# Half of w1's columns contracted in blocks of 128, 128, 96 and 96 rows, with the 96-row blocks loaded in eight transfers of 12 rows

## The chip, the cores and the metric

The kernel runs on one core of one Trainium2 chip. The metric is the device time of one execution in microseconds, the median of the runs. The profile is one further execution, taken by the hardware profiler; its times are microseconds from the first instruction of the program.

## What is computed

One decode step for a batch of two tokens of width 448. A gate mixes the result of a cached attention with that of a small two-layer network:

```python
# x (2,1,448); k_cache, v_cache (2,16,4096,256); w1 (448,1792); w2 (1792,448); all float32
g = sigmoid((x * gate_w).sum(-1, keepdims=True))
q = (x @ wq) in 16 heads of 256
p = softmax(q . k_cache / 16)            # over 4096 cached positions
a = (p . v_cache, heads joined) @ wo
b = maximum(x @ w1, 0) @ w2
out = g * a + (1 - g) * b
```

The two caches hold 268 MB of the 289.5 MB that an execution reads, and each of their values is used once.

## The kernel before

**The ring.** On-chip memory holds a ring of three slots of 16,384 floats in each of 128 partitions. There are 32 units, one for each batch entry and head. A unit's slot holds its K (16 KB x 2 per partition) and V (32 KB per partition). TensorE makes the scores (L131), VectorE takes their maximum (L351), ScalarE the exponentials (L318), and VectorE multiplies them into V in eight instructions (L356), the last of which raises `freed`. SyncE waits for `freed` and issues the load that reuses the slot, so a load is issued as soon as the unit that held its slot is done, some 19 us before its data are due.

**All loads are on SyncE's queue, in one order** (L67 to L178): `wq` with the small input `xg` behind it in slot 0, the units, and then, in slots that are free again, `wm` (w1 and w2) in slot 0 and `wo` in slot 1. `wm` is issued in two transfers, w1 (L170) and w2 (L171), once unit 29 is done; `wo` in six (L175), of 14, 8, 4, 3, 2 and 1 blocks of 448 columns, once unit 30 is done. Each transfer takes all 128 partitions and raises a semaphore of its own by 16.

**w1 in memory.** The 1,792 columns are four groups (g = 0 to 3) of 448. The 448 rows are contracted in three blocks of 128 and a rest of 64. The rest of two groups is stacked in one block of 128 partitions, which one matmul with the input `xl` (x in the upper half for one group, in the lower half for the other, zeros elsewhere) works off for both. So w1 is 14 blocks of 448 floats in each partition, 25,088 bytes, in two halves of seven: groups 0 and 1, then groups 2 and 3.

**The tail on TensorE** (`pe_tail`, L225 to L287) runs in this order: wait for w1 (L231); x times w1, contraction blocks 0 and 1 (`hidden(0, 2)`, recorded on L111, the helper `project`); wait for the last unit; two transposes of the softmax's maxima and sums (L234, L235), which start a chain on VectorE and ScalarE (L361 to L367); block 2 of w1; the weights of the four parts (L238); the rest of w1 (L114); the sum over the parts (L245); the hidden layer transposed (L250, L252); wait for w2, and 14 matmuls with it into `acc` (L258); then for each of the first three `wo` transfers a wait and its matmuls into `acc` (L270). VectorE copies `acc` out (L375), TensorE folds the copy into `z` (L278), adds the last three `wo` transfers there directly, a wait for each (L283), and VectorE copies `z` to `res` (L377), which SyncE stores (L178).

**The inputs of the first matmuls** are made by ScalarE from `xg` once `wq` has landed: `xr` (L297), `xn` (L298) and `xl` (L301). The last raises `x_ok`, for which TensorE's first instruction waits. `xg` is a few columns behind `wq` in the same rows: 4 blocks of 3 columns.

Of the kernel before, what the change touches and what calls it, by code (L numbers as in the profile page):

```python
# [4 lines left out]
AF = mybir.ActivationFunctionType  # L5
# [12 lines left out]

def gated_mix_decode(nc, wq, kv, wm, wo, out):
    U, _, SW = kv.shape  # L20
# [9 lines left out]
    HH = H // G  # L30
    NW = wq.shape[1] - KC * (B + 1)
    FG = 448
    NF = 14
    W1 = 2 * (2 * KF * FG + FG)
    DG = D // G
# [40 lines left out]
    xl = sb("xl", P, 2, RB, B)  # L76
    xn = sb("xn", P, P // B, B)
    ge = sb("ge", P, 1)
    gp = sb("gp", P, 1)
# [25 lines left out]
    def x_of(c, n=R):  # L105
        return xr[:, c].rearrange("p r b -> p (r b)")[:, :n]
# [10 lines left out]

    xg = slot[0][:, NW:wq.shape[1]].rearrange("p (c b) -> p c b", c=KC)

# [27 lines left out]
    w1 = slot[0][:, :W1]  # L147
    w2 = slot[0][:, W1:W1 + NF * D]
    w_o = slot[1]

    with nc.Block(no_gpsimd_drain=True) as block:

        @block.sync
        def _(_e):
            sp.wait_ge(q_mm, 2)
            sp.dma_start(slot[0], kv[2]).then_inc(slot_in[0], 16)
            with nc.Fori(0, LOOP - 2, engines=(ET.SP,)) as r:
                u0 = sp.snap(r * SLOTS)
                for k in range(SLOTS):
                    s = (k + 1) % SLOTS  # L160
                    sp.wait_ge(freed, u0 + k + 1)
                    sp.dma_start(slot[s], kv[bass.ds(u0 + k + SLOTS, 1)].rearrange("o p n -> (o p) n")  # L162
                                 ).then_inc(slot_in[s], 16)
            sp.wait_ge(freed, U - 4)
            sp.dma_start(slot[1], kv[U - 2]).then_inc(slot_in[1], 16)
            sp.wait_ge(freed, U - 3)
            sp.dma_start(slot[2][:, :SW // 2], kv[U - 1][:, :SW // 2]).then_inc(slot_in[2], 16)
            sp.dma_start(slot[2][:, SW // 2:], kv[U - 1][:, SW // 2:]).then_inc(last_v, 16)
            sp.wait_ge(freed, U - 2)
            sp.dma_start(w1, wm[:, :W1]).then_inc(w1_in, 16)  # L170
            sp.dma_start(w2, wm[:, W1:]).then_inc(w2_in, 16)  # L171
            sp.wait_ge(freed, U - 1)
            k = 0
            for n, s in zip(ACC + DIRECT, wo_in):
                sp.dma_start(w_o[:, k * D:(k + n) * D], wo[:, k * D:(k + n) * D]).then_inc(s, 16)  # L175
# [49 lines left out]
        def pe_tail():  # L225
            half = W1 // 2
            def hidden(lo, hi):
                return project(pa, w1, lambda c, g: g // 2 * half + (g % 2 * KF + c) * FG,
                               lambda i: i * half + 2 * KF * FG, FG, lo, hi)

            pe.wait_ge(w1_in, 16)  # L231
            hidden(0, 2)
# [62 lines left out]
        def _(_e):  # L295
            act.wait_ge(slot_in[0], 16)
            act.activation(xr, xg[:, :KF, None, :B].to_broadcast([P, KF, P // B, B]), AF.Copy)  # L297
            act.activation(xn, xg[:, KF:, :B].to_broadcast([P, P // B, B]), AF.Copy)  # L298
            act.wait_ge(xl_0, 1)
            for j in range(2):  # L300
                a = act.activation(xl[j * HP:(j + 1) * HP, j], xg[j * HP:(j + 1) * HP, KF:, :B]  # L301
                                   .to_broadcast([HP, RB, B]), AF.Copy)
# [135 lines left out]
```

## Time and profile before

| | |
|---|---|
| median of 3 runs | 676.2 us (675.98 to 676.47) |
| the profiled execution's own time | 676.38 us |
| its span, first to last instruction | 674.8 us |
| read from memory | 289.54 MB, 429 GB/s over the span |
| packets of the kernel's transfers, share of 16 DMA engines | 99.3% |
| VectorE, TensorE, ScalarE busy | 339.8, 213.0, 54.2 us |

The span leaves 1.6 us of the profiled execution's time outside it. In the profile, a name such as `ring<-in_wm` is a tile and what it is made from; `L170` is a line of the kernel; "128*32 128x448" is the shape of a weight load (128 partitions by 32 columns) and of what is streamed through it. A float32 matmul of the program is recorded as two. SPq rows are SyncE issuing a transfer. In brackets stands how long the engine was idle before, and whose end released it. DMA packets are the pieces that the 16 DMA engines move one after the other; a transfer also leaves a packet of a few bytes on each engine, which raises the semaphore.

### The profile page before, as it was taken

What the parts mean: (1) busy time and instruction counts of PE and PEld (TensorE: products, weight loads), DVE (VectorE), ACT (ScalarE), POOL (GpSimd) and SP (SyncE); (2) the same over time, 40 slices, a digit from 0 to 9 for tenths busy, and PEclk for the clock granted to TensorE, in tenths of its full rate; (3) what the DMA queues carried; (4) which work ended last, traced back from release to release, by engine and by line L of the source; (5) the groups of instructions that cost most, each with busy time, mean ns of one, the idle gap of its engine ahead of it and who ended that gap; (6) DMA issues with size and microseconds to landing.
All of it is one profiled execution on the core that took longest, in us unless ns stands there. A gap on an engine that the chain in (4) does not pass through costs nothing.

```text
span 674.8 us, 4173 instructions
## 1 busy us (share of the span) xinstructions
PE 213.0 (32%) x1279; PEld 52.0 (8%) x1279; DVE 339.8 (50%) x561; ACT 54.2 (8%) x144; POOL 1.1 (0%) x9
## 2 busy tenths in 40 slices
PE   0633221333332123333321233333222333332455
PEld 0210000000000000000000000000000000000011
DVE  0024566545455665544656654455566445456670
ACT  0110000000000000000000000000000000000110
POOL 0000000000000000000000000000000000000000
PEclk9976567767655676776656677665667767655879
DMA  9999999999999999999999999999999999999997
GB/s 381 427 435 436 435 435 435 435 435 435 435 435 435 435 435 435 435 435 435 431 435 435 435 435 435 435 435 435 435 435 435 435 435 435 435 435 406 420 437 304
DMA packets 6082, 289.59 MB, mean 429 GB/s; under 512 B 704, under 2 KB 832, under 8 KB 1216
## 3 DMA queue, kind: packets, MB, share of 16 engines
q1 hardware_dynamic: 6080, 289.55, 99.3%
q8 instruction: 2, 0.03, 0.0%
HBM read 289.54 MB, written 0.01 MB: 429 GB/s over the span
## 4 chain that ended last, share of the span: by engine, by line
DMA 70%; DVE 12%; PE 9%; issue 6%; DVEq 1%; ACT 1%; SPq 0%; ACTq 0%
DMA ring<-in_kv 65%; DVE ring L356 10%; PE sc L131 9%; DMA ring<-in_wo 4%; DVE nm L351 2%; DVEq L356 1%; ACT p L318 1%; PE z L283 0%; DVEq L348 0%; DVEq L353 0%; PE acc L270 0%; SPq L175 0%; SPq L162 0%; DVEq L351 0%; DVE a_sb L375 0%
## 5 line engine op out<-in xcount | busy, mean ns | idle before, releaser
L356 DVE SCALAR_TENSOR_TENSOR ring<-ring,p 128x1024 f32 x256 | 295.9, 1222 | 54.8 <-ACT p L318 54.8
L131 PE MATMUL sc<-ring,qc 128*32 128x512 f32 x1024 | 182.6, 878 | 417.8 <-DMA ring<-in_kv 417.8
L351 DVE TENSOR_REDUCE nm<-sc 128x1024 f32 x32 | 39.2, 1225 | 236.1 <-PE sc L131 236.1
L131 PEld LDWEIGHTS sc<-ring,qc 128*32 128x32 f32 x1024 | 41.2, 154 | 558.6 <-issue 558.6
L318 ACT ACTIVATE p<-sc,nm 128x1024 f32<-128x1024 f32 x32 | 35.7, 1114 | 257.8 <-DVE nm L351 257.8
L323 ACT ACTIVATE ov<-on 128x8 f32 x32 | 6.7, 208 | 309.0 <-DVE ring L356 309.0
L356 DVE DVE_READ_ACCUMULATOR ring<-ring,p 128x1 f32 x256 | 21.4, 83 | 0.0
L343 DVE TENSOR_SCALAR ge<-ge 128x1 f32<-128x1 f32 x1 | 0.2, 155 | 21.5 <-ACT ge L305 21.5
L196 PE MATMUL pa<-ring,xr 128*128 128x1 f32 x6 | 1.4, 356 | 21.4 <-ACT xl L301 21.4
L375 DVE COPY a_sb<-acc 128x448 f32<-128x448 f32 x1 | 0.6, 625 | 14.7 <-PE acc L270 14.7
L111 PE MATMUL pa<-ring,xr 128*32 128x448 f32 x24 | 4.2, 830 | 11.7 <-DMA ring<-in_wm 11.7
L270 PE MATMUL acc<-ring,oc 128*32 128x448 f32 x52 | 5.9, 544 | 4.7 <-DMA ring<-in_wo 4.7
L111 PE MATMUL pb<-ring,xr 128*32 128x512 f32 x48 | 7.1, 737 | 0.0
L318 ACT ACTIVATION_READ_ACCUMULATOR p<-sc,nm x32 | 6.2, 193 | 0.0
L320 ACT ACTIVATE qc<-qt x32 | 6.1, 192 | 0.0
L258 PE MATMUL acc<-ring,hr 128*32 128x448 f32 x28 | 3.2, 541 | 1.0 <-ACT hr L332 1.0
L196 PEld LDWEIGHTS pa<-ring,xr 128*128 128x128 f32 x6 | 1.4, 326 | 21.4 <-ACT xl L301 21.4
L270 PEld LDWEIGHTS acc<-ring,oc 128*32 128x32 f32 x52 | 1.7, 109 | 8.9 <-issue 5.9
L114 PE MATMUL pb<-ring,xl 128*64 128x512 f32 x8 | 2.2, 618 | 0.0
L297 ACT ACTIVATE xr<-ring 128x384 f32<-128x384 f32 x1 | 0.5, 522 | 18.3 <-DMA ring<-in_wq 18.3
L111 PEld LDWEIGHTS pb<-ring,xr 128*32 128x32 f32 x48 | 1.6, 132 | 3.9 <-issue 3.9
L308 ACT ACTIVATE q<-pb 128x512 f32<-128x512 f32 x2 | 1.2, 598 | 8.6 <-PE pb L114 8.6
(56 smaller groups left out, 23.7 us busy)
## 6 DMA issues: line engine op xcount, KB each, us to landing
ring<-in_kv SPq DMA_DIRECT2D x2, 4096.0 KB, 34.7
ring<-in_wq SPq DMA_DIRECT2D x1, 7174.0 KB, 19.5
ring<-in_wm SPq DMA_DIRECT2D x2, 3136.0 KB, 30.7
ring<-in_wo SPq DMA_DIRECT2D x1, 3136.0 KB, 24.4
ring<-in_wo SPq DMA_DIRECT2D x1, 1792.0 KB, 28.3
ring<-in_wo SPq DMA_DIRECT2D x1, 896.0 KB, 30.0
ring<-in_wo SPq DMA_DIRECT2D x1, 672.0 KB, 31.1
ring<-in_kv SPq DMA_DIRECT2D x31, 39.6
```

The costliest lines, as they stand in the source:

```text
L111: m = pe.matmul(dst[g * R:(g + 1) * R, :n], x_of(c), w[:, at(c, g):at(c, g) + n], start=(c == 0), stop=False)
L114: m = pe.matmul(dst[i * HP:(i + 1) * HP, :n], xl.rearrange("p j r b -> p (j r b)"), w[:, at_last(i):at_last(i) + n], start=False, stop=True)
L131: m = pe.matmul(sc[g * R:(g + 1) * R, c * CW:(c + 1) * CW], qc[:, s, t:t + 1].to_broadcast([P, R]), slot[s][:, lo:lo + CW], start=(t == 0) ...
L196: m = pe.matmul(pa[:, :1], x_of(c, P) if c < KF else xn[r].rearrange("p r b -> p (r b)"), xg[r, c, B:], start=(c == 0), stop=(c == KC - 1))
L258: pe.matmul(acc[g * R:(g + 1) * R, :D], hr[:, k, :], w2[:, k * D:(k + 1) * D], start=(k < G), stop=False)
L270: m = pe.matmul(acc[g * R:(g + 1) * R, :D], o_of(k), w_o[:, k * D:(k + 1) * D], start=False, stop=(k >= n - G))
L308: act.activation(q, pb, AF.Copy, scale=SCALE).then_inc(q_ok, 1)
L318: act.activation(p, sc, AF.Exp, bias=nm[:, bass.ds(u, 1)], accum_out=ls[:, bass.ds(u, 1)]).then_inc(raised, 1)
L320: act.activation(qf[:, bass.ds((u + 2) % SLOTS * T, T)], qt[:, bass.ds(u + 1, 1), :].rearrange("p o t -> p (o t)"), AF.Copy).then_inc(quer ...
L323: act.activation(ov[:, bass.ds(u, 1), :].rearrange("p o j -> p (o j)"), on, AF.Copy).then_inc(kept, 1)
L351: dve.tensor_reduce(nm[:, bass.ds(u, 1)], sc, axis=AX.X, op=ALU.max, negate=True).then_inc(maxed, 1)
L356: m = dve.scalar_tensor_tensor(v, v, 1.0, p, op0=ALU.mult, op1=ALU.mult, accum_out=on[:, j:j + 1])
```

## The change

Groups 0 and 1 stay as they were. For groups 2 and 3 the 448 rows are contracted as 128 + 128 + 96 + 96. The two blocks of 128 stay in `wm`; the 96-row blocks of both groups, four blocks of 448 floats in each of 96 partitions, become a new input `we`. It is loaded behind w1 in eight transfers: transfer j brings 12 rows of 7,168 bytes to the partitions j, j + 8, ..., j + 88. All nine transfers raise `w1_in`, and TensorE waits for all nine ahead of its first matmul with w1. The bytes in total stay the same: w1's row goes from 25,088 to 19,712 bytes in 128 partitions, and 96 rows of 7,168 bytes are added. In memory, the rows of `we` that go to the partitions 8r to 8r + 7 lie 44,800 bytes apart, which is also the new pitch of `wm`, and the next eight start 9 x 44,800 bytes on.

A matmul of a 96-row block streams 96 partitions. The contraction's second-last block is rows 256 to 351, which are in `xr` already; the last, rows 352 to 447, needs a new input tile `xe`. It is one more instruction on ScalarE ahead of `x_ok`, from three more columns of `xg`, so `wq`'s rows grow from 57,392 to 57,404 bytes.

```diff
-    NW = wq.shape[1] - KC * (B + 1)
+    NW = wq.shape[1] - (KC + 1) * (B + 1)
-    W1 = 2 * (2 * KF * FG + FG)
+    PS = 96
+    W1 = 2 * KF * FG + FG + 4 * FG
+    WE = 4 * FG
...
     w1 = slot[0][:, :W1]
-    w2 = slot[0][:, W1:W1 + NF * D]
+    w1e = slot[0][:PS, W1:W1 + WE]
+    w2 = slot[0][:, W1 + WE:W1 + WE + NF * D]
...
             sp.wait_ge(freed, U - 2)
             sp.dma_start(w1, wm[:, :W1]).then_inc(w1_in, 16)
+            for j in range(8):
+                sp.dma_start(w1e[j::8], we[:, j, :WE]).then_inc(w1_in, 16)
             sp.dma_start(w2, wm[:, W1:]).then_inc(w2_in, 16)
...
         def pe_tail():
-            half = W1 // 2
+            half = 2 * KF * FG + FG
+
             def hidden(lo, hi):
-                return project(pa, w1, lambda c, g: g // 2 * half + (g % 2 * KF + c) * FG,
-                               lambda i: i * half + 2 * KF * FG, FG, lo, hi)
-
-            pe.wait_ge(w1_in, 16)
+                for c in range(lo, hi):
+                    for g in range(G):
+                        i, h = divmod(g, 2)
+                        if i == 0 and c == KF:
+                            if g == 0:
+                                pe.matmul(pa[:HP, :FG], xl.rearrange("p j r b -> p (j r b)"),
+                                          w1[:, 2 * KF * FG:half], start=False, stop=True)
+                            continue
+                        x, at = x_of(c) if c < KF else xe.rearrange("p r b -> p (r b)"), (h * KF + c) * FG
+                        if i:
+                            at = half + (h * 2 + c) * FG if c < 2 else (h * 2 + c - 2) * FG
+                        w = w1e if i and c >= 2 else w1
+                        m = pe.matmul(pa[g * R:(g + 1) * R, :FG], x[:PS] if w is w1e else x, w[:, at:at + FG],
+                                      start=(c == 0), stop=(c == KC - 1))
+                return m
+
+            pe.wait_ge(w1_in, 9 * 16)
             hidden(0, 2)
...
             act.activation(xr, xg[:, :KF, None, :B].to_broadcast([P, KF, P // B, B]), AF.Copy)
-            act.activation(xn, xg[:, KF:, :B].to_broadcast([P, P // B, B]), AF.Copy)
+            act.activation(xn, xg[:, KF:KC, :B].to_broadcast([P, P // B, B]), AF.Copy)
+            act.activation(xe, xg[:, KC:, :B].to_broadcast([P, RB, B]), AF.Copy)
...
+    both = w1[:2 * P, 1].reshape(2, P, 2, FG).transpose(1, 2, 0, 3).reshape(P, -1)
+    rest = w1[2 * P:, 1].reshape(2, PS, 2, FG).transpose(1, 2, 0, 3).reshape(PS // 8, 8, -1)
+    we = np.zeros((PS // 8, 9, 25 * FG), np.float32)
+    we[:, :8, :rest.shape[2]] = rest
+    w1 = np.concatenate([full, last, both], 1)
```

More of the change, by code (lines that the diff above doesn't have):

```diff
@@ L16, with gated_mix_decode @@
 DIRECT = (3, 2, 1)
-def gated_mix_decode(nc, wq, kv, wm, wo, out):
+def gated_mix_decode(nc, wq, kv, wm, we, wo, out):
     U, _, SW = kv.shape
@@ L77, in gated_mix_decode @@
     xn = sb("xn", P, P // B, B)
+    xe = sb("xe", P, RB, B)
     ge = sb("ge", P, 1)
@@ L116, in project @@
         return m
-    xg = slot[0][:, NW:wq.shape[1]].rearrange("p (c b) -> p c b", c=KC)
+    xg = slot[0][:, NW:wq.shape[1]].rearrange("p (c b) -> p c b", c=KC + 1)
     ident_0, ident_ok, par_ok, fold_ok, xl_0 = (ev() for _ in range(5))
@@ L297, in _ @@
             act.activation(xr, xg[:, :KF, None, :B].to_broadcast([P, KF, P // B, B]), AF.Copy)
-            act.activation(xn, xg[:, KF:, :B].to_broadcast([P, P // B, B]), AF.Copy)
+            act.activation(xn, xg[:, KF:KC, :B].to_broadcast([P, P // B, B]), AF.Copy)
+            act.activation(xe, xg[:, KC:, :B].to_broadcast([P, RB, B]), AF.Copy)
             act.wait_ge(xl_0, 1)
             for j in range(2):
-                a = act.activation(xl[j * HP:(j + 1) * HP, j], xg[j * HP:(j + 1) * HP, KF:, :B]
+                a = act.activation(xl[j * HP:(j + 1) * HP, j], xg[j * HP:(j + 1) * HP, KF:KC, :B]
                                    .to_broadcast([HP, RB, B]), AF.Copy)
@@ L404 @@
     full, last = blocks(np.concatenate([np.asarray(A_x).reshape(B, D).T, np.asarray(gate_w).reshape(D, 1)], 1))
-    xg = np.concatenate([full, np.concatenate([last, last])[:, None]], 1)
+    PS = 96
+    ext = np.zeros((P, 1, B + 1), np.float32)
+    ext[:PS, 0] = np.concatenate([full[PS:, KF - 1], last])
+    xg = np.concatenate([full, np.concatenate([last, last])[:, None], ext], 1)
     kt = np.asarray(A_k_cache)[:, heads].reshape(B, H, S, T, P).transpose(1, 0, 4, 3, 2).reshape(U, P, T * S)
@@ L416 @@
     wo = np.asarray(A_wo).reshape(HH, G, R, J, D).transpose(1, 2, 0, 3, 4).reshape(P, -1)
-    full, last = blocks(B_w1)
-    full = full.reshape(P, KF, 2, 2, FG).transpose(0, 2, 3, 1, 4).reshape(P, 2, -1)
-    last = last.reshape(HP, 2, 2, FG).transpose(2, 0, 1, 3).reshape(P, 2, FG)
-    w1 = np.concatenate([full, last], 2).reshape(P, -1)
+    w1 = np.asarray(B_w1).reshape(D, 2, 2, FG)
+    full, last = blocks(w1[:, 0])
+    full = full.reshape(P, KF, 2, FG).transpose(0, 2, 1, 3).reshape(P, -1)
+    last = last.reshape(HP, 2, FG).transpose(1, 0, 2).reshape(P, FG)
+    both = w1[:2 * P, 1].reshape(2, P, 2, FG).transpose(1, 2, 0, 3).reshape(P, -1)
[3 more added lines that the diff above has]
+    w1 = np.concatenate([full, last, both], 1)
     w2 = np.asarray(B_w2).reshape(G, FG, D)
@@ L424 @@
     w2 = np.concatenate([full, last], 1).reshape(P, -1)
-    arrays = {"wq": wq, "kv": kv, "wm": np.concatenate([w1, w2], 1), "wo": wo}
+    arrays = {"wq": wq, "kv": kv, "wm": np.concatenate([w1, w2], 1), "we": we, "wo": wo}
     arrays = {n: np.ascontiguousarray(a) for n, a in arrays.items()}
```

## The prediction

> **What bounds the kernel now.** I read the page first (engines, slices, DMA packets, chain), then the chain of waits at the end, then windows over the last two microseconds.
>
> ```profile
> GB/s 381 427 435 436 435 435 435 435 435 435 435 435 435 435 435 435 435 435 435 431 435 435 435 435 435 435 435 435 435 435 435 435 435 435 435 435 406 420 437 304
> DMA packets 6082, 289.59 MB, mean 429 GB/s; under 512 B 704, under 2 KB 832, under 8 KB 1216
> q1 hardware_dynamic: 6080, 289.55, 99.3%
> DMA 70%; DVE 12%; PE 9%; issue 6%; DVEq 1%; ACT 1%; SPq 0%; ACTq 0%
> ```
>
> The transfers run without a gap: 99.3% of sixteen engines, 435 GB/s in nearly every slice, 27.2 GB/s for each engine. So the bytes that the busiest engine carries, and what follows its last one, set the time. The 6,080 packets also tell how a transfer is cut. There are 43 transfers; 42 of 128 rows and the output of 16 rows make 5,392 packets if a row is one packet, and 43 x 16 = 688 small ones raise the semaphores: 6,080. One row is one packet, on one engine.
>
> ```profile
> 639.02 29.95 DMA ring<-in_wo
> ...
> 669.02 1.00 PE acc L270 x8
> 670.02 0.02 issue
> 670.05 0.64 DVE a_sb L375
> 670.68 0.04 issue
> 670.73 0.40 PE z L278 x8
> 671.12 1.53 PE z L283 x48
> ```
>
> The end waits for transfers twice: for the third piece of `wo` (to 668.98), and inside the last group (L283) for the last pieces. If all pieces land earlier or later by the same amount, the end moves by that amount.
>
> ```profile
> core 0: us, PE busy (x) PEld busy (x) DVE busy (x) ACT busy (x) POOL busy (x), PEclk, DMA share, GB/s
> 16.87:320.00 303.13, 98.37 (x552) 24.06 (x552) 148.41 (x242) 25.10 (x67) 0.00 (x0) 0.67 1.01 435
> 670.00:670.50 0.50, 0.00 (x0) 0.00 (x0) 0.45 (x1) 0.00 (x0) 0.00 (x0) 1.00 0.64 244
> 670.50:671.40 0.90, 0.67 (x28) 0.68 (x32) 0.17 (x1) 0.00 (x0) 0.00 (x0) 1.00 0.12 48
> 671.40:672.00 0.60, 0.60 (x27) 0.37 (x20) 0.00 (x0) 0.00 (x0) 0.00 (x0) 1.00 0.05 18
> ```
>
> The DMA share is the number to look at. At 670.5 most engines have ended. Until 671.4 it is 0.12, two engines of sixteen; after that 0.05, one engine for the larger part of the window. So fourteen engines end near 670.5, one at 671.4, one at 671.9: the last one is 1.4 us late, and the kernel waits for it. What makes two engines late shows in the DMA view of two short windows, 60 to 66 us and 659 to 661.5 us, the only ones with a packet of another queue:
>
> ```profile
> q8 instruction: 1, 0.02, 1.0%
> ...
> q8 instruction: 1, 0.02, 2.4%
> ```
>
> Each is a fetch of instructions, 1.0% of 16 x 6 us and 2.4% of 16 x 2.5 us, so 0.96 us of one engine, and the data behind it moves back by that or more. Two fetches, two late engines: I take the one as the cause of the other. The view doesn't number the engines.
>
> **The change, part by part.**
>
> ```profile
> ring<-in_wo SPq DMA_DIRECT2D x1, 3136.0 KB, 24.4
> ring<-in_wo SPq DMA_DIRECT2D x1, 1792.0 KB, 28.3
> ring<-in_wo SPq DMA_DIRECT2D x1, 896.0 KB, 30.0
> 638.18 2.70 SPq L175 DMA_DIRECT2D ring<-in_wo  x6
> L170 SPq DMA_DIRECT2D ring<-in_wm x1: 328/328/328, 620.0 to 620.0; - x1
> L171 SPq DMA_DIRECT2D ring<-in_wm x1: 432/432/432, 620.4 to 620.4; - x1
> DMA to landing us min/median/max: 27.2/30.7/34.3
> ```
>
> *Bytes on each engine.* w1 and w2, 3,136 KB each, land (34.3 - 27.2) + 0.4 = 7.5 us apart. The 896 KB piece of `wo` has rows of 7,168 bytes, eight on each engine; it lands 30.0 - 28.3 plus the 0.43 us between two issues = 2.13 us behind the piece before it. w1 shrinks to 19,712 of 25,088 bytes: 7.45 x 0.214 = 1.6 us less on every engine. `we` is eight transfers of twelve packets. A transfer of twelve packets can use twelve engines at most. If it is always the same twelve, each gets eight rows of 7,168 bytes, +2.13 us, net +0.55 us, and the other four are left at -1.6 us. [...]
>
> *Do twelve rows land at full speed?* Every load in this trace fills all 128 partitions, so no row prices one that fills twelve. When only two engines are left (670.5 to 671.4) they move 48 GB/s, 24 each, with fourteen others idle: an engine doesn't get faster when the rest are silent. So the limit is a lane of its own, the engine or the place in on-chip memory where it writes, and the row can't say which. Lower bound: the engine is the limit, and a packet takes what the 896 KB piece shows, 2.13 us for eight. Upper bound: the place is the limit, and two rows of a transfer share one place: twice that, +2.13 us. I take a value near the upper end, +2.0 (engines are some tenths of a microsecond apart, as the 0.64 in 670.0 to 670.5 shows, and two that meet a little apart share a little less). What decides me is that the rate stands at 435 GB/s to within 1 in nearly every slice: every lane is full at both ends, with no spare seen in the place of landing. [...]
>
> *The end.* The twelve: 670.5 + 0.55 + 2.0 = 673.05. The two late engines, if both are among the spared four: 671.9 - 1.6 = 670.3, not last any more. The end moves by 673.05 - 671.9 = +1.2 us.
>
> *Work that hides.*
>
> ```profile
> SPq L175 <- DVE ring L356: 17.4, 1, 17.4
> 647.26 3.21 PE L111 MATMUL pa<-ring,xr 128*32 128x448 f32 x16 [11.73 <-DMA ring<-in_wm]
> 650.40 0.40 PE L234 MATMUL pc<-ident,nm 128*32 128x128 f32 x1
> 650.94 1.01 PE L111 MATMUL pa<-ring,xr 128*32 128x448 f32 x8
> 652.62 0.97 PE L114 MATMUL pa<-ring,xl 128*64 128x448 f32 x4
> 656.25 3.20 PE L258 MATMUL acc<-ring,hr 128*32 128x448 f32 x28 [1.01 <-ACT hr L332]
> 662.72 3.20 PE L270 MATMUL acc<-ring,oc 128*32 128x448 f32 x28 [3.27 <-DMA ring<-in_wo]
> 39.72 5.51 PE L131 MATMUL sc<-ring,qc 128*32 128x512 f32 x32 [4.65 <-DMA ring<-in_kv]
> 20.71 0.29 ACT L298 ACTIVATE xn<-ring 128x128 f32<-128x128 f32 x1
> ```
>
> Eight more issues on SyncE, 8 x 0.43 = 3.5 us, stand between w1 and w2 at 620; w2's data are due 25 us later, and the next thing on that queue is `wo`, ahead of which SyncE waits 17.4 us. Cost 0. If that wait were under 3.5 us, `wo` would be late by the difference.
>
> The wait of L231 now ends with the last row of `we`, 0.55 us later by bytes alone, 2.55 with shared landing, less what late engines had cost it: 647.3 becomes about 648.7. Behind it on TensorE are the 3.2 us of `hidden(0, 2)` and the two transposes (L234, L235) for which the softmax chain on VectorE and ScalarE waits; they move from 650.4 to some 652. `w2` lands up to 2.5 us later on the twelve engines, and before 657, about when the hidden layer is ready. The rest of w1 takes one more matmul, two records of 0.13 to 0.25 us (L111 x8 took 1.01, L114 x4 0.97), at most 0.5 us. In sum TensorE comes to L270 up to 2.2 us later, and there it has 3.27 us of idle time in front of `wo`, which itself moves by 1.2. Cost 0. Were that cover gone, the excess over 3.27 + 1.2 us would be added to the end.
>
> `xe` is one more ScalarE instruction, 0.2 to 0.3 us like L298, ahead of all of TensorE's work; the first unit then has 4.65 us to spare before its data. 12 bytes more in 57,392 cost nothing that can be seen.
>
> Sum against the profiled execution: 676.38 + 1.2 = 677.6. Its time is 0.18 above the median of 676.2, so the forecast is 677.4.
>
> **The rivals.**
>
> *Full speed, late engines spared.* The engine is the limit, and twelve rows land at full speed. The twelve end at 670.5 + 0.55 = 671.05, the spared late ones at 670.3: -0.85, of which extra semaphore packets (eight for one) take about 0.1. 675.45. For it: no row shows two engines disturbing each other. Against it: no row shows a lane with room. The case turns to the forecast when the eight packets take over 0.85 us more than 2.13.
>
> *Shared landing, and the last engine isn't spared.* The later of the two is one of the twelve: 671.9 + 0.55 + 2.0, +2.6 us, 678.8. For it: nothing numbers the late engines, and three in four are not spared if they fall anywhere. Against it: only that both fetches come over one queue, so that the two late engines may well be neighbours.
>
> *Full speed, the last engine isn't spared:* +0.55, 676.75.
>
> *The rows are dealt round all sixteen engines.* Then each gets six rows, as many bytes as before; the change moves nothing that counts: 676.2.
>
> **How the numbers follow.** The rule for twelve engines I give 0.93. Shared landing against full speed I put at about 2 to 1 in its favour. That the last engine is spared I put at over three quarters, above the one in four of a blind draw, because the two fetches came over one queue and so aren't two separate draws; no row carries that number, and it is the weakest step. So: shared and spared 0.48, full and spared 0.24, shared and not spared 0.15, full and not spared 0.06, dealt round 0.07.
>
> A measurement of this kernel tells about 0.2% from no change, 1.35 us: under 674.85 or over 677.55. The forecast lies 0.15 us inside; I count 0.43 of its 0.48 chance as slower, 0.21. With 0.14 of the third case, slower is 0.35. Faster needs more than the whole 1.4 us of lateness back: 0.04. The rest, 0.61, is within. The likeliest case's own range is 676.9 to 677.9. The range of 8 in 10 runs from 675.3 (full speed) to 678.6 (most of the case not spared).
>
> **What would show it.** In the windows of the changed kernel the DMA share stays high past 671.0 and falls in two steps, the pairs last, near 673. The GB/s row falls from 437 in its second-last slice (641 to 658), in which `we` lands. w1's wait ends near 648.7. If instead the share is near zero at 671.1, full speed holds; if one engine alone remains to 674, the last engine wasn't spared; if the end of transfers looks as before, 0.12 then 0.05, the rows were dealt round. An idle time before L270 that isn't released by `wo` would break the step that TensorE's tail is covered. A change over 3 us either way would mean a mechanism that I don't have.

## The result and the profile after

The changed kernel takes 679.37 us, median of 7 runs (677.19 to 680.71), beside 676.2 us (7 runs, 675.98 to 677.05) for the kernel before on the same chip. The ratio is 1.0043, with a 95% interval of 1.0028 to 1.0058: slower by about 2.9 us. The forecast was 677.4 us with a range up to 678.6.

The traced execution, however, came out nearly as forecast by its span: 675.7 us, 0.9 above the 674.8 of before (forecast +1.2). Its own time is 678.44 us, with 2.7 us outside the span where before's trace has 1.6. First the page of the changed kernel, the same rows that the prediction shows of before:

```profile
GB/s 381 431 434 432 434 434 434 434 434 434 434 434 434 434 434 434 434 434 434 434 434 434 434 434 434 434 434 434 434 434 434 434 434 434 434 434 433 422 380 326
DMA packets 6274, 289.59 MB, mean 429 GB/s; under 512 B 800, under 2 KB 928, under 8 KB 1408
q1 hardware_dynamic: 6272, 289.56, 99.4%
DMA 68%; DVE 12%; PE 11%; issue 6%; DVEq 1%; ACT 1%; SPq 0%; ACTq 0%
```

The second-last slice, where `we` lands, is down from 437 to 380 GB/s; the first 36 slices are within 4 GB/s of before. The 192 packets more are 96 rows and 8 times 12 semaphore packets. Twelve and not sixteen: there are 96 more under 512 B than before (800 for 704), so each of the eight transfers leaves twelve semaphore packets where one of 128 rows leaves sixteen. I read that as twelve engines.

Windows of the changed kernel, one before `we`, one in it, and four at the end (columns: busy time of each engine with the number of instructions, granted clock, DMA share, GB/s):

```profile
637.70:643.50 5.80, 0.00 (x0) 0.00 (x0) 4.09 (x8) 1.50 (x4) 0.00 (x0) 0.65 1.01 434
643.90:647.40 3.50, 0.00 (x0) 0.00 (x0) 3.50 (x7) 0.00 (x0) 0.00 (x0) 0.50 1.20 288
...
670.00:671.00 1.00, 0.87 (x8) 0.06 (x8) 0.06 (x1) 0.00 (x0) 0.00 (x0) 1.00 0.91 371
671.00:672.00 1.00, 0.39 (x16) 0.39 (x20) 0.56 (x1) 0.00 (x0) 0.00 (x0) 1.00 0.85 339
672.00:672.40 0.40, 0.40 (x26) 0.34 (x16) 0.00 (x0) 0.00 (x0) 0.00 (x0) 1.00 0.66 251
672.40:673.00 0.60, 0.60 (x24) 0.35 (x16) 0.00 (x0) 0.00 (x0) 0.00 (x0) 1.00 0.04 15
```

Read the last two columns together. A window counts a packet whole where it starts, so a share can pass 1; what tells is the rate for the busy share. It is 288 / 1.20 = 240 GB/s while `we` lands and 434 / 1.01 = 430 ahead of it: the packets take longer. This is what the prediction called shared landing. At the end, before had one or two engines left from 670.5 to 671.9; now most of them run to 672.4 and then stop, with one engine 0.3 us behind (0.04). So in this execution the late engines were spared, as forecast, and the twelve end last, at 672.4 instead of the forecast 673.05. Part of that is luck: the packets of the last unit ended some 0.4 us earlier in this execution than in before's trace.

The trace keeps every DMA packet with its start, length and size, and they say more than the windows. On one engine a packet starts within some 5 ns of the end of the one before it, so the packets can be sorted into sixteen chains, one for each engine. A row of `we` takes 272 ns on its engine at first, and 420 to 550 once all twelve engines are at it. But the four engines that carry no row of `we` slow down as well: their first packets of w2 take up to 1.78 us in place of 0.93. So the rows hinder other transfers too, and not only each other two by two within one, as the prediction had it. By this the two late engines, forecast to end at 670.3, end at 671.6 and 671.9, as late as in before; they are only not the last any more.

The tail on TensorE and the third piece of `wo`, from the timeline of the changed kernel:

```profile
648.98 3.21 PE L247 MATMUL pa<-ring,xr 128*32 128x448 f32 x16 [14.09 <-DMA ring<-in_we]
...
663.64 3.20 PE L290 MATMUL acc<-ring,oc 128*32 128x448 f32 x28 [1.59 <-DMA ring<-in_wo]
667.78 1.71 PE L290 MATMUL acc<-ring,oc 128*32 128x448 f32 x16 [0.94 <-DMA ring<-in_wo]
669.91 0.96 PE L290 MATMUL acc<-ring,oc 128*32 128x448 f32 x8 [0.42 <-DMA ring<-in_wo]
...
673.61 0.28 DVE L398 COPY res<-z 128x112 f32<-128x112 f32 x1 [2.05 <-PE z L303]
```

w1 is ready at 648.98 (forecast 648.7, before 647.26). The idle time ahead of `wo` shrinks from 3.27 to 1.59 us but is still ended by `wo`: TensorE's tail stays covered. The third piece starts at 669.91 instead of 669.02, 0.89 us later, and what follows it takes as long as before (to 673.61, +0.93 against 672.68). That is the whole difference of the traced spans.

Most of the other executions are longer than the traced one. The spans of the seven runs are 675.7 (traced), 677.7, 675.5, 678.8, 677.5, 678.0 and 679.1 us. So the question for the experiments was not what the trace shows, but what makes five executions of seven 1.8 to 3.4 us longer than it.

### The profile page after: what moved, and what is told of

It is laid out like the page before. It is cut to its first block, busy times and chain, and to the rows that moved or that the text cites. A ratio compares the mean times of both kernels' runs of the same rounds, so it can differ in the third digit from the quotient of the medians.

```text
span 675.7 us, 4186 instructions
## 1 busy us (share of the span) xinstructions
PE 214.6 (32%) x1281; PEld 52.4 (8%) x1281; DVE 339.8 (50%) x561; ACT 54.3 (8%) x145; POOL 1.1 (0%) x9
## 3 DMA queue, kind: packets, MB, share of 16 engines
q1 hardware_dynamic: 6272, 289.56, 99.4%
## 4 chain that ended last, share of the span: by engine, by line
DMA 68%; DVE 12%; PE 11%; issue 6%; DVEq 1%; ACT 1%; SPq 0%; ACTq 0%
DMA ring<-in_kv 64%; PE sc L134 10%; DVE ring L377 10%; DMA ring<-in_wo 4%; DVE nm L372 2%; DVEq L377 1%; ACT p L339 1%; PE z L303 0%; DVEq L369 0%; DVEq L374 0%; PE acc L290 0%; SPq L181 0%; SPq L166 0%; DVEq L372 0%; DVE a_sb L396 0%
## 5 line engine op out<-in xcount | busy, mean ns | idle before, releaser
L247 PE MATMUL pa<-ring,xr 128*32 128x448 f32 (+1 forms) x24 | 4.4, 854 | 14.1 <-DMA ring<-in_we 14.1
L290 PE MATMUL acc<-ring,oc 128*32 128x448 f32 x52 | 5.9, 544 | 2.9 <-DMA ring<-in_wo 2.9
L290 PEld LDWEIGHTS acc<-ring,oc 128*32 128x32 f32 x52 | 1.7, 109 | 7.1 <-issue 4.2
L393 DVE COPY oc<-pc 128x256 f32<-128x256 f32 x4 | 1.4, 416 | 1.5 <-PE pc L265 1.5
```

Of the source, the lines that this page charges most:

```text
L247: m = pe.matmul(pa[g * R:(g + 1) * R, :FG], x[:PS] if w is w1e else x, w[:, at:at + FG], start=(c == 0), stop=(c == KC - 1))
L290: m = pe.matmul(acc[g * R:(g + 1) * R, :D], o_of(k), w_o[:, k * D:(k + 1) * D], start=False, stop=(k >= n - G))
```

## The experiments

Four explanations were tried against each other. The expectations number or letter them as they came up, and put them in words: that landing is shared and the late engines are spared in every execution (the forecast); that the late engines sit on other engines from one execution to the next, so that the credit for sparing them is earned in some executions alone (called Theory 4 later on); that shared landing itself scatters; and that the cost isn't in the loads at all but in TensorE's longer program, through a third fetch of instructions near the end (called Theory A). Each row of the table is one kernel beside the kernel before on the same chip; "third piece" is the start of the third `wo` group in the timeline of its trace, and "idle" the idle time ahead of the first, as in the rows above. The kernel before had medians of 676.2 to 676.5 us on these chips.

| kernel | median us (range, runs) | ratio, 95% interval | w1 ready | idle | third piece | traced span |
|---|---|---|---|---|---|---|
| before | 676.2 (675.98 to 677.05, 7) | | 647.26 | 3.27 | 669.02 | 674.8 |
| the changed kernel | 679.37 (677.19 to 680.71, 7) | 1.0043 (1.0028 to 1.0058) | 648.98 | 1.59 | 669.91 | 675.7 |
| again | 680.21 (678.19 to 681.18, 6) | 1.0054 (1.0042 to 1.0066) | 648.94 | 1.72 | 670.00 | 676.9 |
| one96 | 679.3 (678.19 to 680.24, 5) | 1.004 (1.0027 to 1.0053) | 649.06 | 1.25 | 670.00 | 675.8 |
| nine | 678.62 (676.64 to 679.77, 12) | 1.0027 (1.0017 to 1.0038) | 648.27 | 0.22 | 669.31 | 675.1 |
| before_plus | 676.18 (675.79 to 676.96, 11) | 0.9999 (0.999 to 1.0008) | 646.96 | 1.53 | 668.57 | 674.3 |
| after_short | 680.23 (677.52 to 680.97, 6) | 1.0051 (1.0036 to 1.0066) | 649.02 | 1.73 | 670.02 | 675.9 |
| nine_short | 678.55 (676.86 to 679.77, 7) | 1.0031 (1.002 to 1.0042) | 648.35 | 0.34 | 669.41 | 675.2 |
| one96_short | 678.57 (677.77 to 679.02, 6) | 1.0031 (1.0019 to 1.0043) | 649.36 | 0.16 | 670.28 | 676.5 |
| native64 | 676.64 (675.3 to 678.45, 11) | 1.0008 (0.9997 to 1.0018) | 647.58 | 1.31 | 668.57 | 674.4 |
| shared64 | 677.73 (676.33 to 681.73, 12) | 1.0029 (1.0013 to 1.0045) | 648.10 | 1.39 | 669.27 | 675.3 |
| contig12 | 680.3 (678.88 to 681.53, 5) | 1.0066 (1.0053 to 1.0079) | 650.49 | none | 671.47 | 677.3 |
| before_xe | 676.66 (675.94 to 677.53, 11) | 1.0006 (0.9997 to 1.0015) | 646.98 | 3.24 | 668.70 | 674.5 |

### The changed kernel once more (again, again2)

No edit. It tells how firm the result is on another chip, and whether another trace shows the same end.

> The changed kernel once more, for its scatter (677.2 to 680.7 us in seven runs; the kernel before 676.0 to 677.1). Theory 1, shared landing and late engines: the twelve engines are slowed in the same way each time, and the time depends on whether the two late engines (behind a fetch of instructions) are among the four spared: levels near 677.2, and 1.4 and 2.8 us above it. Theory 2, shared landing alone: the slowing itself differs from run to run, so no levels, and in a slow execution all twelve engines end late together.

> The changed kernel, for a second trace. Theory 1: if its span is over 677, one engine alone ends last, 1 us or more behind the rest. Theory 2: if its span is over 677, the twelve engines end together and the window of the 12-row transfers is longer than the 3.5 us of the first trace.

The ratio is 1.0054: the cost is there again, and larger. The spans are 676.9 (traced), 677.2, 678.9, 677.4, 677.7 and 678.1 us. The second trace, again2, is one execution of 677.93 us with a span of 675.5. In both traces the third piece starts at 670.00 and 669.62, as in the first: three traces in three show a short execution. In the trace of again, the DMA view of the last stretch (674.0 to 676.9 us) has a packet of the other queue, which in the first trace comes only after the last instruction, at 677.4 us:

```profile
q8 instruction: 1, 0.02, 2.0%
...
out<-res SPq DMA_DIRECT2D x1, 7.0 KB, 2.8
```

2.0% of 16 x 2.9 us is 0.93 us of one engine. It is a third fetch of instructions; the store of the output, which took 1.8 us in the first trace, takes 2.8 here behind it. That is 1.0 of the 1.2 to 1.4 us by which this span is longer than the first's and again2's, and it gave Theory A.

### One transfer of 96 rows (one96)

```diff
-            for j in range(8):
-                sp.dma_start(w1e[j::8], we[:, j, :WE]).then_inc(w1_in, 16)
+            sp.dma_start(w1e, we).then_inc(w1_in, 16)
...
-            pe.wait_ge(w1_in, 9 * 16)
+            pe.wait_ge(w1_in, 2 * 16)
```

Sixteen engines with six rows each: the bytes on each engine are those of before, and everything else is the change.

> The same matmuls, but the 96 rows in one transfer, so that all sixteen engines take six rows each. Theory 1 and 2: no engine has more bytes than before, and rows of different engines meet less, so 676.2 to 676.8 us and a scatter as small as before. Rival, the contraction itself costs (one more matmul, xe, the later wait): still 677.5 us or more.

A miss: 679.3, as slow as the changed kernel. Its timeline shows w1 ready as late as there:

```profile
649.06 3.21 PE L246 MATMUL pa<-ring,xr 128*32 128x448 f32 x16 [13.86 <-DMA ring<-in_we]
```

So 96 partitions are dear even when sixteen engines carry them. The run shows that the bytes alone don't explain the cost; what makes 96 partitions dear isn't shown. Here no engine is spared (the DMA share is 1.00 from 670 to 671 us), and the late ones are last again, with two engines left after the others:

```profile
671.60:672.70 1.10, 0.97 (x33) 0.74 (x33) 0.05 (x1) 0.00 (x0) 0.00 (x0) 1.00 0.12 49
```

### Twelve rows nine partitions apart (nine)

```diff
-    PS = 96
+    PS = 107
...
-                sp.dma_start(w1e[j::8], we[:, j, :WE]).then_inc(w1_in, 16)
+                sp.dma_start(w1e[j:j + 100:9], we[:, j, :WE]).then_inc(w1_in, 16)
...
-            act.activation(xe, xg[:, KC:, :B].to_broadcast([P, RB, B]), AF.Copy)
+            act.activation(xe, xg[:, KC:, None, :B].to_broadcast([P, 2, RB, B]), AF.Copy)
```

The same twelve engines and bytes; rows r and r + 4 are now 36 partitions apart instead of 32. The inputs `xe` have zeros in the partitions between.

> Eight transfers of 12 rows as in the change, the same twelve engines and bytes, but partitions nine apart (j, j + 9, ...), with x placed to match and zeros between. If two rows of a transfer share a landing place at a distance of 32 partitions, this parts them: a packet takes its 272 ns, the window of these rows moves over 380 GB/s in place of 288, and the end comes 1.5 to 2 us earlier than with the change: 675.4 us where the late engines are spared, 676.8 where one is not. If the number of engines alone decides, the time is that of the change, 679.4.

678.62: 0.75 us below the first measurement of the changed kernel, 1.6 below again on the same chip, and 2.1 above before. w1 is ready 0.71 us earlier (648.27). Half a step: the distance matters, and it isn't the whole. The twelve spans fall in two heaps: 675.0 to 675.7 us (five, the traced one among them) and 676.5 to 678.5 (seven). That is what a cost would look like that is there in some executions and not in others.

### Is it TensorE's program? (before_plus, after_short, nine_short, one96_short)

To the kernel before, one product is added whose result the next one overwrites, so that its program gets longer:

```diff
             hidden(2, KF)
+            pe.matmul(z[:R, :FG], x_of(0), w1[:, :FG], start=True, stop=True)
             pe.wait_ge(wb_ok, 1)
```

And from three kernels six instructions of TensorE are taken out (the tile `hs` is widened to 512 columns, and ScalarE fills the new ones with one instruction more):

```diff
-            for t in range(KF):
-                pe.transpose(pb[:, t * P:(t + 1) * P], hs[:, t * P:(t + 1) * P], ident)
-            for j in range(2):
-                m = pe.matmul(pb[j * HP:(j + 1) * HP, KF * P:], hs[:, KF * P:], ident, start=True, stop=True)
+            for t in range(KC):
+                m = pe.transpose(pb[:, t * P:(t + 1) * P], hs[:, t * P:(t + 1) * P], ident)
```

> The kernel before, with one matmul more in TensorE's tail (four instructions: two weight loads, two matmuls), whose product is overwritten; loads as before. Theory A, length of TensorE's program: the change's extra matmul makes it long enough that a third page of instructions is fetched at the end, as the traces of all the changed kernels have it (674.8 to 677.4 us) and that of before has not; then this one has the third fetch, 677.5 to 680 us and a scatter of 3 us. Theory B, the loads of the 96 rows cost all: two fetches, 676.5 us.

> The change with TensorE's program made six instructions shorter, two fewer than before: two matmuls that transpose the hidden layer's last columns are replaced by one transpose, with a second ScalarE instruction that writes these columns twice. Theory A: no third fetch, and what is left is the price of the twelve engines that share landing places, +0.9 us by the first trace: 677.2 us, scatter under 1.5 us. Theory B: no difference to the change, 679.4 to 680.2.

> Partitions nine apart and the shorter program. Theory A: no third fetch, and the span of the first trace with nine apart (675.1) less nothing: 676.5 us, within 0.2% of before. Theory B: as nine apart alone, 678.6.

> All 96 rows in one transfer over sixteen engines and the shorter program. Theory A: 676.2 to 677 us, as before. Theory B: as one transfer alone, 679.3.

before_plus costs nothing (0.9999, 0.999 to 1.0008), though its trace does have the third fetch. The DMA view from 675.0 to 676.8 us, of the longer program:

```profile
DMA packets 1, 0.02 MB, mean 9 GB/s; under 512 B 0, under 2 KB 0, under 8 KB 0
...
q8 instruction: 1, 0.02, 3.3%
```

It comes here behind the output's store and delays nobody. And the three shortened kernels are as slow as their originals: 680.23, 678.55 and 678.57 beside 679.37, 678.62 and 679.3, all with ratios of 1.003 to 1.005. But taking out six instructions did not take out the third fetch: all three traces still have it. The DMA view of after_short from 672 to 680 us:

```profile
q8 instruction: 1, 0.02, 1.1%
```

So these three kernels don't try Theory A. What speaks against it as the whole cost is before_plus, and the loads alone further down, which have no fetch and cost nearly as much more (+2.56 us). That a third fetch which comes early costs some executions 1 us, as in again, stays.

### The same engines and bytes, rows four and eight partitions apart (native64, shared64)

Groups 2 and 3 are contracted as 128, 128, 128 and 64 rows. The 64 rows of 3,584 bytes come in eight transfers of eight rows, so eight engines carry 1.05 us more and w1 takes 0.53 less on all. The two kernels differ in one line, the distance of the rows of a transfer, four or eight partitions (and in the order of the rows in memory):

```diff
-                sp.dma_start(w1e[j // 4 * 32 + j % 4:j // 4 * 32 + j % 4 + 29:4], we[:, j, :WE]).then_inc(w1_in, 16)
+                sp.dma_start(w1e[j::8], we[:, j, :WE]).then_inc(w1_in, 16)
```

> Another split: groups 2 and 3 contracted as 128, 128, 128 and 64, the 64 rows (of 3,584 bytes) loaded in eight transfers of 8 rows four partitions apart. Eight engines carry 0.57 us more, eight 0.53 us less, and no two rows of a transfer lie 32 partitions apart. Theory 3, where landing places are shared the slowing is large and uneven, and that is the scatter: here nothing is shared, so 675.6 to 676.4 us with the scatter of before. Theory 4, it is the place of the late engines that changes from run to run: two levels, 0.5 us under and 0.6 us above before.

> [...] Theory 3: eight packets of 0.14 us take twice, +1.1 us or more on top of the run with four apart, and the scatter of the change. Theory 4: one step of +1.1 us, two levels. If landing places don't matter: no difference to four apart.

676.64 and 677.73: with the same engines, bytes, packets and instructions, rows that are eight apart cost 1.1 us more in the median, and the runs reach up to 681.73 instead of 678.45. The two intervals just overlap; the traces and the loads alone below say the same. w1 is ready 0.52 us later, the third piece 0.70. A window in the stretch in which the rows land, native64 first:

```profile
643.50:647.50 4.00, 0.00 (x0) 0.00 (x0) 4.00 (x9) 0.00 (x0) 0.00 (x0) 0.50 1.07 453
```

and shared64:

```profile
643.50:647.50 4.00, 0.00 (x0) 0.00 (x0) 4.00 (x9) 0.00 (x0) 0.00 (x0) 0.50 1.00 347
```

For the busy share that is 347 instead of 423 GB/s: packets that take longer, by nothing but the places where they land. In native64's loads alone every row takes 140 ns; in shared64's trace up to 270.

native64 is the only one of the kernels with a new split of w1 whose time is not told from before. Its spans are 673.9 to 674.4 us (five), 675.0 to 675.4 (four) and 676.8 (two). In its loads alone no row takes more than 140 ns, so steps between executions have another cause here. The place of the late engines is one candidate, an early third fetch another; this run doesn't part them.

### Twelve neighbours, and the inputs alone (contig12, before_xe)

```diff
-                sp.dma_start(w1e[j::8], we[:, j, :WE]).then_inc(w1_in, 16)
+                sp.dma_start(w1e[12 * j:12 * j + 12], we[:, j, :WE]).then_inc(w1_in, 16)
```

> The change with each transfer's 12 rows in 12 neighbouring partitions. If four neighbouring partitions are one landing place, four rows share one, and eight packets take 4 x 2.15 = 8.6 us in place of 4.3: the end of transfers moves by about 4 us, 683 us. If the number of engines decides, 679.4 as the change.

The slowest of all, 680.3, but far from the 683 expected for four rows in one place: its span is 677.3, 1.6 over the changed kernel's. The window over the landing of the rows:

```profile
637.00:650.00 13.00, 0.00 (x0) 0.00 (x0) 11.29 (x18) 1.50 (x4) 0.00 (x0) 0.61 0.99 294
```

294 GB/s over these 13 us, where the changed kernel has 356. And here the idle time ahead of `wo` is gone: TensorE comes to L290 when its data are there. From there the pieces still pace it (0.95 and 0.42 us of idle time ahead of the second and third), so it costs nothing yet.

before_xe is the kernel before with `xe`, its instruction on ScalarE and the 57,404-byte rows of `wq`, and nothing else of the change:

> The kernel before with the change's three more columns behind wq (rows of 57,404 bytes) and the one more ScalarE instruction, which nothing reads; w1 as before. All theories: 676.4 us, as before. If it is 677.5 or more, the longer rows or the later start cost.

676.66, ratio 1.0006 (0.9997 to 1.0015). These parts cost nothing that can be told, as forecast.

### The loads alone (bare_before, bare_after)

All computing is left out, and the output is zeros: the same loads in the same order, each issued when the load that held its slot has landed, and the output stored once all have landed.

```diff
-                sp.wait_ge(freed, u - 1)
+                sp.wait_ge(slot_in[s], 16 * ((u + 1) // SLOTS))
                 sp.dma_start(slot[s], kv[u]).then_inc(slot_in[s], 16)
...
+            dve.memset(res, 0.0).then_inc(res_ok, 1)
```

The pages of both kernels show no packet of the instruction queue. So no engine is late by a fetch, and the bytes and their landing are all that is left.

> The loads of the kernel before alone, in its order, each as soon as its slot's last load has landed; all compute is left out and the output is zeros. No engine's program is long enough for fetches of instructions. Both theories: the transfers end without late engines, some 1.4 us earlier after the last byte than with compute, so 671 to 673 us with the tail's compute gone, and a scatter under 1 us.

> The loads of the change alone, in the same way. Theory 3 (the sharing of landing places is itself uneven): 2.5 us over the bare loads of before in the best run, and a scatter of 2 to 4 us above that. Theory 4 (the scatter comes from where the late engines fall): without fetches no engine is late, nothing is gained from sparing four, so 2.5 us (0.55 of bytes, 2.0 of sharing) over the bare loads of before in every run, and a scatter as small as theirs.

673.95 (673.79 to 674.25, 5 runs) and 676.51 (676.27 to 679.67, 11 runs): +2.56 us. The forecast had 0.55 for bytes and 2.0 for shared landing. The windows at the end of bare_before:

```profile
669.00:669.50 0.50, 0.00 (x0) 0.00 (x0) 1.00 0.97 376
669.50:670.00 0.50, 0.00 (x0) 0.00 (x0) 1.00 0.62 233
670.00:670.50 0.50, 0.00 (x0) 0.00 (x0) 1.00 0.00 0
```

and of bare_after:

```profile
671.00:672.00 1.00, 0.00 (x0) 0.00 (x0) 1.00 0.74 299
672.00:672.50 0.50, 0.00 (x0) 0.00 (x0) 1.00 0.69 262
672.50:673.00 0.50, 0.00 (x0) 0.00 (x0) 1.00 0.02 7
```

In the first, no single engine is left behind the others (compare 0.12 and 0.05 in the prediction's rows): without fetches there are no late engines. In the second, twelve of sixteen (0.75) run on until 672.5 and stop together. There is one more thing in the runs: eight of the eleven lie within 676.27 and 676.67, and three at 678.5, 679.52 and 679.67. With no engine computing and no fetch, a program of loads takes 2 to 3 us longer in some executions. Theory 4 forecast 2.5 us in every run; the three long ones are what Theory 3 forecast.

### Where the late engines sit, and which loads scatter (load8, bare_native64, bare_shared64, bare_nine)

load8 is the kernel before with four transfers more, of eight rows of 15,360 bytes four partitions apart, as in native64 (453 GB/s while they land), into columns that nobody reads; TensorE waits for them with w1:

```diff
             sp.dma_start(w1, wm[:, :W1]).then_inc(w1_in, 16)
+            for j in range(4):
+                sp.dma_start(slot[0][j:j + 29:4, SW - 3840:], wm[8 * j:8 * j + 8, :3840]).then_inc(w1_in, 16)
             sp.dma_start(w2, wm[:, W1:]).then_inc(w2_in, 16)
```

Eight engines get 61,440 bytes more, 2.26 us at 27.2 GB/s, and eight get nothing. If the late engine, 1.4 us behind, is one of the eight others, the end moves by 2.26 - 1.4 = 0.86 us; if it is one of the loaded, by the whole 2.26.

> The kernel before with four transfers of 8 rows of 15,360 bytes behind w1, into a part of slot 0 that nothing reads, rows four partitions apart so that none share a place: eight engines carry 4 x 0.57 = 2.27 us more, the other eight nothing. Theory 4 (the late engines' places change from execution to execution): levels 1.4 us apart, 677.3 (both late engines among the unloaded: 670.5 + 2.27 against 671.9), 678.7 (one loaded), 680 (both late on one loaded engine), the low one in about a quarter of the runs and in the traced one. If the late engines always sit where the traces have them: 677.3 in every run, with the scatter of before.

677.5 (676.83 to 678.65, 11 runs), ratio 1.0015 (1.0006 to 1.0024). The kernel before has a median of 676.66 on this chip, and 676.66 + 0.86 = 677.52: the time is that of late engines which always sit on the unloaded side, and the scatter, 1.8 us beside 1.6, is nearly that of before. The spans are 675.2, 675.2, 675.6, 675.7, 675.8, 675.9, then 676.6, 676.8, 676.9, 677.3, and the traced 676.4. By the median span of before, 674.6, Theory 4's two lower levels are due at 675.4 and 676.8. That fits the spans as well, but the traced one shows another way to an upper level: a third fetch. The DMA view of its last stretch (673.5 to 676.4 us):

```profile
q8 instruction: 1, 0.02, 2.3%
...
out<-res SPq DMA_DIRECT2D x1, 7.0 KB, 2.9
```

Its output's store took 2.9 us for the 1.8 without. So the spans of load8 don't decide for Theory 4. The traces speak against it. Here is the end of load8's, with the columns as before:

```profile
670.00:671.00 1.00, 0.35 (x4) 0.00 (x0) 0.58 (x1) 0.00 (x0) 0.00 (x0) 1.00 0.62 251
671.50:671.80 0.30, 0.30 (x21) 0.30 (x16) 0.00 (x0) 0.00 (x0) 0.00 (x0) 1.00 0.48 185
672.30:673.50 1.20, 0.78 (x24) 0.32 (x16) 0.27 (x1) 0.00 (x0) 0.00 (x0) 1.00 0.00 0
```

Ten engines run at first, the eight loaded and two more; then eight; and all stop by 672.3. Had a late engine been one of the loaded eight, it would have run on alone for another 1 us. The same in the trace of again, with twelve loaded: two engines of sixteen are through by 670.9, fourteen run on, and nothing is left behind the twelve.

```profile
670.90:671.80 0.90, 0.15 (x8) 0.10 (x8) 0.62 (x1) 0.00 (x0) 0.00 (x0) 1.00 0.84 341
672.90:674.00 1.10, 0.73 (x24) 0.29 (x16) 0.28 (x1) 0.00 (x0) 0.00 (x0) 1.00 0.00 0
```

The chains of packets make it exact. In before, the engine that made the fetch at 63 us ends at 671.4, the one that made the fetch at 659.8 ends at 671.9 (the packet behind that fetch took 1.40 us instead of 0.93), and the other fourteen at 670.2 to 670.5. So the fetches are what makes the two engines late, as the prediction took it. There are ten traces of kernels that leave some engines with less to carry: four engines in the changed kernel, again, again2, nine, after_short, nine_short and contig12, eight in native64, shared64 and load8. In all ten, both engines that fetch are among those. If their places were drawn anew in each execution, one trace of the first seven would show that with a chance of 1 in 20. So in the traced executions the late engines are spared every time; of the untraced ones only spans are known.

The other three are the loads of native64, shared64 and nine alone, as above with no computing and zeros as output.

> The loads alone of the split with 64 rows, four partitions apart; compute left out, output zeros. Bytes alone: eight engines carry 0.57 us more, 674.5 us, and no run far above, since no places are shared and no fetches make an engine late. If runs 2 us and more above the rest appear as in the bare loads of the change (3 of 11), sharing isn't what makes them.

> The loads alone of the split with 64 rows, rows eight partitions apart; everything but the distance as in the bare loads four apart (674.75 us, 674.46 to 675.12). Sharing of places: eight packets of 0.14 us take twice, +1.1 us, 675.9, and now and then a run 2 us or more above that, as in the bare loads of the change. If distance doesn't matter: 674.75.

> The loads alone of the variant with 12 rows nine partitions apart. If nine apart parted all twelve rows, bytes alone: 674.5 us. If the rows still meet those of other engines, which write their usual places meanwhile, something between 674.5 and the 676.5 of eight apart.

| loads alone | median us (range, runs) | over bare_before | by bytes alone |
|---|---|---|---|
| bare_native64 | 674.75 (674.46 to 675.12, 8) | +0.80 | +0.53 |
| bare_shared64 | 675.5 (675.12 to 675.87, 11) | +1.55 | +0.53 |
| bare_nine | 676.03 (675.83 to 679.78, 12) | +2.08 | +0.55 |
| bare_after | 676.51 (676.27 to 679.67, 11) | +2.56 | +0.55 |

The rows were measured on three chips (bare_before and bare_after on one, native64 on another, shared64 and nine on a third), on which the kernel before differs by up to 0.3 us. Eight apart for four costs 0.75 us with the same engines and bytes. Nine apart for eight gives back 0.5 of bare_after's 2.0, so most of the 2.0 isn't the distance of eight partitions: twelve rows nine apart still cost 1.5 us over their bytes. The trace of bare_nine shows where: its rows take up to 550 ns for 272, and w2's packets on the four other engines up to 1.72 us for 0.93, so the rows hinder those of other transfers and are hindered. Three of bare_nine's twelve runs are at 678.71, 678.82 and 679.78, as three of bare_after's eleven; the loads with eight rows have no such run in 19, four or eight apart. With the computing, however, shared64 has them too (spans of 678.1, 679.5 and 679.8 us among its twelve), while the eight-row transfers with rows four apart, native64 and load8, have none above 677.3 in 22. So the third explanation is the one that the runs bear out: the long executions come with the transfers that get in each other's way. What happens in a long execution isn't shown, as none was traced.

## Why the prediction was wrong

**What bounds the kernel: right.** The loads run without a gap (99.4% of sixteen engines in the changed kernel, 99.3% in before), and the span ends 5.8 us behind the start of the third piece of `wo` in the changed kernel as in before. Where a third fetch stands ahead of the output's store it is more, 6.9 us in again.

**Bytes on each engine: right.** Twelve engines and +0.55 us by bytes; the number of packets shows the twelve, and the loads alone show the sum of this and the next term. That all eight transfers take the same twelve (the "rule for twelve engines" of the chances) was an assumption, which no row of before shows; in the changed kernel's trace four engines carry no row of `we`, and in bare_after's the DMA share is 0.74 and 0.69 from 671 to 672.5 us, about twelve of sixteen.

**Shared landing at +2.0 us in every execution: the step that failed.** The size is right for the short executions: 0.55 + 2.0 was forecast, and bare_after measured +2.56 in the median. But the prediction took one price for all executions, with twice the row's time, +2.13, as its upper bound, and put the scatter at nothing without a reason. With no computing and no fetch, eight runs of bare_after lie 2.3 to 2.7 us over bare_before and three lie 4.6 to 5.7 over it: less 0.55 for bytes, a landing of 1.8 to 2.2 us, and of 4.0 to 5.2 in three executions of eleven. The forecast with these 2.1 to 3.3 us more gives 679.5 to 680.7. Five of the changed kernel's seven runs lie at 679.35 to 680.71, the other two at 677.19 and 678.44, about the forecast. The sizes agree; that the long executions of the whole kernel are the same thing as those of its loads is argued, and why they are five of seven here and three of eleven there stays open.

The mechanism was right in part. That two rows of a transfer share one place, from which the upper bound and with it the +2.0 were worked out, was an assumption that no run shows as such. In its place the runs show that the distance of the rows counts: eight apart for four costs 0.75 us bare and 1.1 with the computing, and nine apart for eight gives back 0.5 (bare) to 1.6 us. The rest, 1.5 us bare, stays with the rows nine apart, and the packets show that other transfers have a part in it: in bare_nine's trace w2's packets on engines without a row of `we` take up to 1.72 us for 0.93 as well.

**Work that hides: right.** `xe` and the longer rows cost nothing (before_xe). TensorE came to the first `wo` group at 663.64 - 1.59 = 662.05 instead of 662.72 - 3.27 = 659.45, 2.6 us later where up to 2.2 was forecast, and the cover held. The issues cost more than forecast: the eight took 6.27 us, 0.78 each instead of 0.43. SyncE still had to wait 12.7 us ahead of `wo`'s issue, by the waits of the changed kernel:

```profile
SPq L181 <- DVE ring L377: 12.7, 1, 12.7
```

**"The two late engines, if both are among the spared four": right in every trace.** It was called the weakest step, and it held. All ten traces have both late engines among those with less to carry. The reason that the prediction gave, one queue for both fetches, was not tried. The size was wrong, though: spared engines were to end 1.6 us earlier, and the slower packets of w2 took that back (671.9 instead of 670.3). The twelve end later still, so it did not matter. Whether an untraced execution ever has a late engine among the twelve isn't shown. The third rival ("the last engine isn't spared", 678.8, which got 0.15) comes nearest to the median of 679.37, but no trace has its sign, an engine that remains alone, so as far as the traces show that nearness is luck.

**The misleading trace.** Every trace of a kernel with twelve-row transfers eight or nine apart (the changed kernel three times, nine, after_short, nine_short) shows one of the shorter executions, and each comes from the first run of its kernel. Had there been only the traced spans, the forecast would have looked right to 0.3 us.

**Open.** What a long execution looks like inside, and what sets it off: none was traced. Why twelve-row transfers have them without computing, and the eight-row transfers of shared64 only with it. Whether the rows of `we` and of w2 meet where they land or already where they are read: that the places of landing decide is shown for the pair native64 and shared64 alone. How much an early third fetch adds: about 1 us in the traces of again and load8, and no kernel here is without it and with the change. Whether the thinner cover ahead of `wo`, 1.59 us and none in again2, makes long executions more frequent: no run tested it. Why contig12 costs only 1.6 us more in its trace. And no version that was tried beats the kernel before: native64 comes nearest, with an interval that holds 1.

## What to carry to other kernels

A forecast of a median needs a term for scatter: look at the spans of many executions and not at one trace, which here showed a shorter one each time. When transfers may get in each other's way, ask what else is landing at the time, and not only what the new transfer does to itself. To tell which engine is late, follow the packets: on one engine each starts where the one before it ends. Taking bytes off some DMA engines by transfers of fewer than 128 rows can have a price in landing, here 1.5 to 2.0 us for 96 rows in the shorter executions and 4 us and more in others, which is to be set against what the spared engines give. To price a transfer, run the loads without the computing: there the kernel before scattered by 0.5 us, and differences of 0.5 to 0.8 us between two layouts could be told.

## What the runs showed of the hardware

- A transfer of twelve rows used twelve DMA engines (192 packets more for eight of them, 96 rows and 96 of the semaphore), and while the eight landed, the rate fell from 434 to 288 GB/s. Packets of w2 on the other four engines took up to 1.78 us meanwhile instead of 0.93.
- The distance of the rows mattered: eight rows eight partitions apart landed at 347 GB/s, four apart at 453, with the same engines.
- Issuing a transfer of twelve rows on SyncE took longer when they lay apart. The issues of `we`, in the changed kernel (twelve rows eight apart), 0.78 us each:

```profile
619.53 6.27 SPq L176 DMA_DIRECT2D ring<-in_we  x8
```

in contig12 (twelve neighbours), 0.41 each:

```profile
619.78 3.24 SPq L176 DMA_DIRECT2D ring<-in_we  x8
```

and in one96 (96 rows, one transfer), 0.43:

```profile
620.18 0.43 SPq L175 DMA_DIRECT2D ring<-in_we  x1
```

- A fetch of instructions took 0.96 us of one DMA engine in before's trace, where the transfers run without a gap, and the two engines that fetched stayed late to the end: 1.1 and 1.6 us behind the middle of the others. In again a fetch stood in front of the output's store, which took 2.8 us instead of 1.8.
- In ten traces of kernels with transfers of twelve or eight rows, the engines that made the two fetches were never among the twelve or eight that carried those rows.
- A program of nothing but loads had executions 2.1 to 3.9 us above the others of the same kernel in 3 of 11 and 3 of 12 runs with twelve-row transfers; with 128-row or eight-row transfers there was none in 24.
